# Inverted sums loaded as sixteen rows, and the order of the memory part changed, in a four-layer attention kernel on one Trainium2 core

## The chip, the cores and the metric

The kernel runs on one NeuronCore of one Trainium2 chip. Its engines are named as the profile names them: PE (TensorE, matmuls; PEld is its weight load), DVE (VectorE), ACT (ScalarE), POOL (GpSimd) and SP (SyncE, which here only issues DMAs). Sixteen DMA engines move data between the chip's memory and the on-chip memories. The metric is the device time of one execution in microseconds; the time before is the median of three executions.

## The reference, cut to what matters

The input x has 2048 tokens of 512 values, split into 32 heads of 16. Four layers run one after the other, A, B, A, B, with one set of weights for both A layers and one for both B layers. Everything is float32.

```python
def _A_ref(x, wqkv, w_phi, wo):            # linear attention
    ...
    phi_q = concatenate([softmax(pq), softmax(-pq)])
    phi_k = concatenate([softmax(pk), softmax(-pk)])
    kv = einsum("bhsf,bhsd->bhfd", phi_k, v); z = einsum("bhsf->bhf", phi_k)
    o = (phi_q @ kv) / (phi_q . z + 1e-6)
    return o @ wo

def _B_ref(x, wq, wk, wv, wo, beta):       # softmax attention in 4 segments with a memory
    ...
    for s in range(4):                     # 512 tokens each
        p = softmax(qs @ ks.T * scale + causal_mask)
        a_dot = p @ vs
        num = phi(qs) @ M;  den = phi(qs) . z + 1e-6
        o_s = g * (num / den) + (1.0 - g) * a_dot
        M = M + phi(ks).T @ vs;  z = z + sum(phi(ks))
    return concat(o_s) @ wo

x = x + A(layernorm(x)); x = x + B(layernorm(x)); x = x + A(layernorm(x)); x = x + B(layernorm(x))
```

An output of a B layer has two parts. The new part `a_dot` comes from the segment's own softmax and is divided by the row sums of the exponentials. The memory part `num / den` comes from the segments before, and is divided by a sum of its own. In the first segment there is no memory yet.

## The kernel before

**Tiles and loops.** Work is laid out with features on the 128 partitions for the B layers: a group `c` of the four groups of eight heads fills 128 partitions (8 heads x 16 features) and the 512 tokens of a segment lie along the free dimension. A B layer is walked by `steps` as 160 numbered steps `k`: 32 half groups `m` (segment `s = m // 8`, group `c = m % 8 // 2`, half `hf = m % 2`), with `R = 5` steps each. In every step `attend` makes one part of the scores of the present half group (PE), `exp` of them (ACT) and the causal mask on the diagonal blocks (POOL, the AFFINE_SELECT instructions on tile P); `maxima` makes row maxima of a later half group (PE into the banks mx and my, DVE); `weighted` makes the products with v (PE into the bank pv, ACT to tile U); `put_maxima` turns the maxima (PE), negates them (ACT) and writes them into the stacked q tile by a DMA that ACT issues (e<-mt).

**The order.** Each engine runs its instructions in the order in which the program emits them (`Ordered`, `held`), and that order is written by hand. The tables FIRST, GAPS, LAST and FINAL (lines 81 to 120) name the filler work of each step: FIRST for segment 0, GAPS for segments 1 and 2, LAST for segment 3 of the first B layer, FINAL for segment 3 of the second. A cell such as `1.3 q3/1~ k3/2` says: in step 3 of half group 1, one quarter of the projection q of group 3 (three matmuls of 512 columns), with the DVE part of its emptying put off into the next step (`~`), then two quarters of k of group 3. `n` normalises and turns rows of the next segment, `out` is the output projection, `x0` to `x3` ask for residual rows (`ask`, tile xr), `max` is `put_maxima`, `v` in LAST is work of the next A layer, and `a1`, `a2`, `a3`, `a0+` are `read` for a group of this or the next segment. TAIL (line 61) is the order of the last pieces of the kernel.

**The sums and their inverses.** For each segment and group, the sums by which outputs are divided are gathered in a DRAM buffer of 16 rows of 512 values (`den`): rows 0 to 7 for the new part of the eight heads (written by `gather`, four rows a half group, from tile U), rows 8 to 15 for the memory part (written by `dens` in `read`, four rows each from the tiles mmq and ot). `invert` then schedules four actions by the table INVERT: `compact` reads the buffer back as a full 128-partition tile (dn with both parts, 64 columns; dm with one part, 32 columns), `flip` takes the reciprocal on DVE, `put` writes it to DRAM (inv), and `load` reads the eight rows of a part back, each repeated for the 16 partitions of its head, as a 128 x 512 tile: KN for the new part, mmq for the memory part.

**The outputs.** `close` is called for a group when its second half is done, with the step number `k` from which the actions are counted, and schedules by the table JOIN: `scaled` (new part times KN, POOL, tmp<-tmp,KN), `scaled_old` (memory part times mmq, POOL, ot<-ot,mmq), `joined` (their sum, POOL, tmp<-tmp,ot), `upper` (ACT, oh<-tmp) and `lower` (POOL, ol<-tmp,oh), the two halves of the number with which the output projection is run. JOIN has one row for segment 0, one for segments 1 and 2, one for segment 3. A whole number of steps is run ahead of the filler of that step, a half one behind it. In segment 3, groups from `cut` = 2 on take another way (`finish`, `end_turn`, `close_last`), and their memory part is scaled by an action set in `read`.

**What `read` does.** It multiplies the memory with phi(q) (PE, into the bank pv and a bank g) and ACT empties the two banks into `old` (tile ot, three buffers) and `upper` (tile mmq, two buffers, which the loads of the memory part's inverses share). The pv bank is a single one, and the next `weighted` needs it.

**Queues.** Nearly all DMAs are issued by SP, in program order; ACT issues e<-mt.

The lines that place `scaled` and its companions are:

```python
            for j, f in zip(JOIN[0 if s == 0 else 2 if s == NSEG - 1 else 1][c], (scaled, scaled_old, joined, upper, lower)):
                if j is not None:
                    self.at(k + j, f)
```

Of the kernel before, what the change touches and what calls it, by code (L numbers as in the profile page):

```python
# [15 lines left out]
D = 512  # L16
H = 32
DH = 16
P = 128
# [29 lines left out]
GATHER = (3.5, 1.5)  # L49
INVERT = (((2.5, 4.5, 5, 7), (2.5, 4.5, 5, 7), (2.5, 4.5, 5, 7), (2.5, 4.5, 5, 7)), ((2.5, 5.0, 5, 7), (2.5, 5.0, 5, 7), (2.5, 5.0, 5, 7), (2.5, 5.0, 5, 7)), ((2.5, 4.5, 5.5, 7.5), (2.5, 4.5, 5.5, 7.5), (2.5, 4.5, 5.5, 7.5), (2.5, 4.5, 5.5, 7.5)))  # L50
READ = (1.5, 2.5, 1, 12.5)
JOIN = (((9.5, None, None, 11, 12.5), (9.5, None, None, 11, 12.5), (9.5, None, None, 11, 12.5), (9.5, None, None, 11, 12.5)), ((9.5, 10.0, 11.5, 12, 13.5), (9.5, 10.0, 11.5, 12, 13.5), (9.5, 10.0, 11.5, 12, 13.5), (9.5, 10.0, 11.5, 12, 13.5)), ((9.5, 11.5, 12.5, 13, 13.5), (9.5, 11.5, 12.5, 13, 13.5), (9.5, 11.5, 12.5, 13, 13.5), (9.5, 11.5, 12.5, 13, 13.5)))
SEAM = 1
QFIRST = False
WARM = 18
# [2 lines left out]
BEGINNING = """  # L58
m0 m1 g0 r0 n0 V0 n1a V1p c0 V2 V3p c1 m2 m3 v1 v1 v1 v1 g1 r1 p n2 k k v1 n3a v1 v1 v1 c2 k k c3 u k v1 v1 v1 K0 K1 K2 K3 v1 u u q q u q u v1 q v1 v1 u u u q Q0 Q2 v1 Q1 u Q3 u u
"""  # L60
TAIL = "p o0 p o1 o2 t0 p p p p o3 t2 P t1 a0 t3 a1 a2 a3"
WEIGHTS = {-2: ((0, (0, 3)), (1, (1, 2))), -1: ((-2, (0,)), (-1, (3, 1)), (0, (2,)))}
SECOND = 9
EARLY = (0, 1, 2)
# [25 lines left out]
"""  # L90
GAPS = """
0.1 max k2/3 | 0.2 n | 0.3 k2/1~ v3/2 | 0.4 a1 v3/2
1.0 m0 n n | 1.1 max q3/3 | 1.2 n | 1.3 q3/1~ k3/2 | 1.4 t1 k3/2~
2.1 max out/3 | 2.2 m1 | 2.3 ln ln | 2.4 a2 ln x0
3.1 max ln out/1~ | 3.3 q0+/3 x1 | 3.4 t2 q0+/1~ k0+/2
4.1 max k0+/2~ out/1 load | 4.2 m2 | 4.3 out/3~ x2 | 4.4 a3 q1+/4~
# [7 lines left out]
1.0 n | 1.1 max q3/3 n | 1.2 n | 1.3 q3/1~ k3/2 n | 1.4 k3/2~ n  # L104
2.1 max out/1 | 2.3 out/2 | 2.4 a2 x0 pre
3.1 max ln~ ln~ | 3.3 pre out/1 ln~ out/1 x1 | 3.4 out/1 ln~
4.1 max out/2~ v/3 | 4.3 pre out/3 x2 | 4.4 a3 out/1~ v/1 x3
5.1 max out/3 | 5.2 out/1 v/1 | 5.3 fin v/1 | 5.4 v/2 pre
6.1 v/2 max | 6.3 fin v/2 | 6.4 v/2
7.1 pt p/3 v/2 | 7.2 v/2 | 7.3 fin v/2 p/3 | 7.4 p/3  # L110
"""
FINAL = """
# [2 lines left out]
2.1 max k3/2 | 2.3 k3/1 out/1 pre | 2.4 a2 out/2 x0  # L115
3.0 x1 | 3.1 max | 3.3 pre out/2 | 3.4 out/2
4.1 max out/1~ | 4.3 pre out/2 x2 | 4.4 a3 out/2
5.1 max out/2 x3 | 5.3 fin out/2 | 5.4 pre
6.1 max | 6.3 fin
7.1 pt p/2 | 7.3 p/4 fin | 7.4 p/3  # L120
"""
# [4 lines left out]
def interleave_kernel(ctx, tc, x_in, a_wqkv, a_wphi, a_wo, b_wq, b_wk, b_wv, b_wo, b_beta,  # L126
# [15 lines left out]
    def nm(s):  # L142
        uid[0] += 1
        return f"{s}_{uid[0]}"

    def T2(tag, bufs, dt=F32, shape=(P, 512)):
        return sp.tile(list(shape), dt, tag=tag, bufs=bufs, name=nm(tag))

    def PS(tag, bufs, shape=(P, 512)):
        return ps.tile(list(shape), F32, tag=tag, bufs=bufs, name=nm(tag))  # L150
# [38 lines left out]
    dve, act, pool, sync = [Ordered(e) for e in (nc.vector, nc.scalar, nc.gpsimd, nc.sync)]  # L189
# [10 lines left out]
    def mm(*a, **k):  # L200
        n = a[0].free_size()
        work[0] += n / 2.26 if k["rhs"].dtype == F32R else (n * 2 / 2.4 + 25 if "tile_position" in k else 2 * max(112, n * 2 / 2.4))
        return held(nc.tensor.matmul(*a, **k))  # L203
# [55 lines left out]
    def dtile(shape, name):  # L259
        return dr.tile(list(shape), F32, name=name)  # L260
# [745 lines left out]
    class LayerB:  # L1006
# [69 lines left out]
        def read(self, s, c, k):  # L1076


            kn, ph = self.summed(s, c)[1], self.st[s, c]["phi", 0]
            pn = [PS("pv", PV), PS("g", G)]  # L1080
            for a in range(2):
                mm(pn[a][0:68, :], lhsT=kn[64 * a : 64 * a + 64, :], rhs=ph[64 * a : 64 * a + 64, :],
                   start=True, stop=True, tile_position=(64 * a, 0))
            old = self.old[s, c] = T2("ot", OT)
            upper = T2("mmq", 2)
            for t, p in zip((old, upper), pn):
                act.activation(t[0:68, :], p[0:68, :], AF.Identity, bias=bd[0:68, 26:27])

            def dens():
                d = self.den(s, c)  # L1090
                for a, t in enumerate((upper, old)):
                    sync.dma_start(out=d[12 - 4 * a : 16 - 4 * a], in_=t[64:68, :])

            def numerators():
                sync.dma_start(out=old[64:128, :], in_=upper[0:64, :])
            self.at(k + READ[0], dens)
            self.at(k + READ[1], numerators)
            if s == NSEG - 1 and c >= self.cut:
                self.invert(s, c, k + READ[2], range(1, 2), INVERT[2][c])

                def scaled():
                    pool.tensor_tensor(out=old, in0=old, in1=self.inv.pop((s, c, 1)), op=MUL)
                self.at(k + READ[3], scaled)

        def den(self, s, c):
            if (s, c) not in self.dens:
                self.dens[s, c] = dtile((16, D), nm("den"))
            return self.dens[s, c]

        def invert(self, s, c, k, parts, steps):  # L1110


            lo, hi = 8 * parts[0], 8 * parts[-1] + 8
            n = (hi - lo) * 4
            tiles = {}

            def compact():
                d = tiles["d"] = T2("dn" if n == 64 else "dm", 1, shape=(P, n))
                sync.dma_start(out=d[:, 0:n], in_=self.den(s, c)[lo:hi].rearrange("h (x i) -> (h x) i", i=n))

            def flip():
                dve.reciprocal(tiles["d"][:, 0:n], tiles["d"][:, 0:n])

            def put():
                tiles["i"] = dtile((hi - lo, D), nm("inv"))
                sync.dma_start(out=tiles["i"].rearrange("h (x i) -> (h x) i", i=n), in_=tiles["d"][:, 0:n])

            def load():
                for i in parts:
                    t = self.inv[s, c, i] = T2(*(("mmq", 2) if i else ("KN", 1)))  # L1130
                    rows = tiles["i"][8 * i - lo : 8 * i - lo + 8].unsqueeze(1).broadcast_to([8, DH, D])
                    sync.dma_start(out=t, in_=rows)
            for j, f in zip(steps, (compact, flip, put, load)):
                self.at(k + j, f)

        def gather(self, s, c, hf, U):
            if hf == 0:
                self.num[s, c] = T2("tmp", 2)
            sync.dma_start(out=self.num[s, c][64 * hf : 64 * hf + 64, :], in_=U[1 - hf : P : 2])
            sync.dma_start(out=self.den(s, c)[4 * hf : 4 * hf + 4], in_=U[31 * hf : P : 32])  # L1140

        def outputs(self, s, c):
            return [T2("oh", OO, F32R), T2("ol", OO, F32R)]
# [1 line left out]
        def close(self, s, c, k):  # L1145
# [19 lines left out]
            def lower():  # L1165
                hi, lo = self.oT[s, c]
                pool.tensor_tensor(out=lo, in0=o, in1=hi.bitcast(F32), op=SUB)
            for j, f in zip(JOIN[0 if s == 0 else 2 if s == NSEG - 1 else 1][c], (scaled, scaled_old, joined, upper, lower)):
                if j is not None:
# [189 lines left out]
        def close_last(self, rest):  # L1359
# [36 lines left out]

            for what in TAIL.split():
                if what == "p":
# [218 lines left out]
    for i in range(2):  # L1617
        lb = LayerB(xs[2 * i + 1], xs[2 * i + 2], CUTS[i], i == 1)
        run(p1[i])
        a2 = la[i].second  # L1620
# [41 lines left out]
```

## Time and profile before

| | us |
|---|---|
| median of three executions | 1423.88 |
| lowest and highest of them | 1420.51 and 1424.61 |
| the profiled execution, whole | 1420.89 |
| its span in the profile | 1419.2 |
| ACT busy, DVE busy, POOL busy | 810.0, 953.1, 733.8 |
| the first B layer, from its first e<-mt to its last output, about | 281 to 716 |
| the second B layer, about | 977 to 1412 |

How to read the profile: a row of the costliest groups has the source line, the engine, the operation, the tiles (out<-in), the shape, the count, then busy time and mean duration in ns, then the engine's idle time ahead of these instructions and what ended most of it. Source lines tell little here, since the helpers on lines 181, 203, 207 and 210 issue nearly everything; the tiles' names tell the instructions apart. A row of the chain of waits has a start, a length and what the time was spent on; a DMA in it counts from its issue to the moment that released the next. A row of the timeline has start, duration, engine, operation, tiles, shape and count, and in brackets the idle time before it and what ended it. A row of busy times by stretch has the stretch, its length, the busy time of PE, PEld, DVE, ACT and POOL with their instruction counts, the granted TensorE clock as a share of full speed, the mean busy share of the sixteen DMA engines, and the rate in GB/s.

### The profile page before, as it was taken

To read this page: it belongs to the slowest core of one execution; us is meant where nothing else is said; L and a number is where in the kernel's file an instruction comes from. 1 tells how busy PE (TensorE), PEld (TensorE's weight loads), DVE (VectorE), ACT (ScalarE), POOL (GpSimd) and SP (SyncE) were. 2 spreads that over 40 slices of the span, in tenths; PEclk is the share of its full clock that TensorE was granted. 3 is DMA by queue.
4 is the path that set the end of the run, shared out by engine and by line. 5 is a ranking of instruction groups with operands and counts; after the bars stand their busy time and mean duration, and the time that the engine had idled before them with its cause. 6 is when DMAs were issued, how large, how long until landed. Compare 5 with 4: busy or idle time off the path is not lost.

```text
span 1419.2 us, 33171 instructions
## 1 busy us (share of the span) xinstructions
PE 1373.8 (97%) x12070; PEld 946.3 (67%) x12070; DVE 953.1 (67%) x3028; ACT 810.0 (57%) x1246; POOL 733.8 (52%) x1073
## 2 busy tenths in 40 slices
PE   9999999999999999999999999999999999999997
PEld 7787778765666565665568887886656565666554
DVE  5766888677666556577546768958776665666663
ACT  5555345447676576566544434553666765765654
POOL 1678765325566556554524446641446565654543
PEclk9999999999999999999999999999999999999999
DMA  5369285536655546466640104854465565555541
GB/s 196 119 220 335 92 267 187 173 115 186 186 132 167 167 133 179 147 162 196 173 146 31 61 31 132 266 177 144 129 185 147 148 182 158 146 165 145 142 143 68
DMA packets 134898, 222.72 MB, mean 157 GB/s; under 512 B 26032, under 2 KB 39472, under 8 KB 134736
## 3 DMA queue, kind: packets, MB, share of 16 engines
q1 hardware_dynamic: 132768, 219.96, 52.0%
q8 instruction: 97, 1.59, 0.5%
q10 hardware_dynamic: 1968, 0.64, 0.2%
q14 instruction: 65, 0.53, 0.1%
HBM read 115.54 MB, written 41.55 MB: 111 GB/s over the span
## 4 chain that ended last, share of the span: by engine, by line
PE 74%; DVE 7%; ACT 6%; DMA 5%; POOL 4%; issue 2%; SPq 1%; ACTq 0%; DVEq 0%; POOLq 0%
PE g L203 45%; PE pv L203 8%; PE lg L203 8%; PE mx L203 4%; PE g L207 3%; ACT P L181 3%; PE my L203 3%; POOL P L181 2%; PE lg L207 2%; DMA e<-ta 1%; SPq L181 1%; DVE es L181 1%; POOL tb L181 1%; POOL tmp L181 1%; DVE junk L181 1%
## 5 line engine op out<-in xcount | busy, mean ns | idle before, releaser
L181 ACT ACTIVATE P<-lg 128x1024 f32<-128x1024 f32 x316 | 324.8, 1028 | 172.5 <-PE lg L203 152.0
L181 POOL TENSOR_SCALAR_AFFINE_SELECT P<-P 128x256 f32<-128x256 f32 (+1 forms) x448 | 190.1, 439 | 399.0 <-ACT P L181 394.8
L181 DVE CUSTOM_DVE_ANT_0 junk<-mx,mask 128x128 uint8<-128x128 f32 (+2 forms) x384 | 147.2, 421 | 116.3 <-PE my L203 86.8
L203 PE MATMUL g<-hh,wqk 128*128 128x512 f32 x512 | 185.2, 410 | 0.7 <-ACT mt L181 0.7
L203 PE MATMUL lg<-e,e 64*128 64x512 f32 (+1 forms) x1010 | 166.3, 387 | 12.3 <-ACT P L181 10.8
L203 PE MATMUL g<-w,oh 128*128 128x512 f32 x508 | 169.5, 414 | 0.5 <-ACT hh L181 0.4
L203 PE MATMUL pv<-P,v 128*32 128x512 f32 (+3 forms) x2048 | 165.1, 439 | 4.4 <-ACT ot L181 4.3
L181 DVE CUSTOM_DVE_ANT_0 mx<-mx,mask 128x512 f32<-128x512 f32 x128 | 89.1, 696 | 114.6 <-PE my L203 93.6
L203 PEld LDWEIGHTS lg<-e,e 64*128 64x128 f32 x1010 | 80.1, 184 | 109.9 <-issue 50.7
L203 PE MATMUL my<-e,e 63*128 63x256 f32 (+3 forms) x519 | 148.1, 345 | 4.3 <-DVE mxs L181 3.2
L203 PE MATMUL mx<-e,e 63*128 63x256 f32 (+3 forms) x519 | 147.0, 336 | 2.2 <-DVE mxs L181 1.9
L181 DVE CUSTOM_DVE_ANT_0 junk<-my,mask 128x128 uint8<-128x128 f32 (+2 forms) x384 | 146.7, 420 | 0.0
L203 PE MATMUL g<-w,hh 128*128 128x512 f32 x448 | 144.0, 402 | 0.3 <-ACT hh L181 0.3
L203 PEld LDWEIGHTS pv<-P,v 128*32 128x32 f32 x2048 | 53.6, 109 | 106.4 <-issue 93.9
L203 PEld LDWEIGHTS g<-hh,wqk 128*128 128x128 f32 x512 | 96.2, 188 | 32.3 <-issue 11.8
L203 PEld LDWEIGHTS g<-w,oh 128*128 128x128 f32 x508 | 87.9, 189 | 30.3 <-issue 13.2
L203 PE MATMUL g<-w,ol 128*128 128x512 f32 x254 | 101.2, 398 | 2.9 <-DVE ol L181 2.1
L203 PE MATMUL g<-hl,wqk 128*128 128x512 f32 x256 | 100.3, 392 | 0.0
L181 DVE DVE_READ_ACCUMULATOR2_ANT mxs<- 128x1 f32 x1024 | 100.1, 98 | 0.0
L203 PEld LDWEIGHTS mx<-e,e 63*128 63x128 f32 (+1 forms) x519 | 90.5, 186 | 11.1 <-DVE mxs L181 4.8
L203 PEld LDWEIGHTS g<-w,hh 128*128 128x128 f32 x448 | 80.3, 188 | 22.9 <-issue 6.3
L203 PEld LDWEIGHTS my<-e,e 63*128 63x128 f32 (+1 forms) x519 | 83.9, 185 | 16.9 <-DVE mxs L181 8.7
(189 smaller groups left out, 2835.9 us busy)
## 6 DMA issues: line engine op xcount, KB each, us to landing
e<-ta SPq DMA_DIRECT2D x384, 128.0 KB
wqk<-wqk SPq DMA_DIRECT2D x64, 512.0 KB
x<-x SPq DMA_DIRECT2D x48, 256.0 KB
xr<-x SPq DMA_DIRECT2D x32, 256.0 KB
x<-xr SPq DMA_DIRECT2D x28, 256.0 KB
tmp<-U SPq DMA_DIRECT2D x56, 128.0 KB
KN<-inv SPq DMA_DIRECT2D x28, 256.0 KB
pq<-tb SPq DMA_DIRECT2D x24, 256.0 KB
```

The source lines that it names most:

```text
L181: i = f(*a, **k)
L203: return held(nc.tensor.matmul(*a, **k))
L207: return held(nc.tensor.transpose(*a))
```

## The change

Four things are changed.

1. The buffer of sums holds each row twice (16 x 2 x 512): the writes of `gather` and `dens` repeat their source rows, `compact` and `put` move tiles of twice the width (dn of 128 columns, dm of 64), `flip` inverts twice as many values, and `load` reads sixteen rows, each repeated for eight partitions, where it read eight rows, each repeated for sixteen.
2. In JOIN `scaled_old` moves from 10.0 to 9.5 for segments 1 and 2, which puts it directly behind `scaled`, and from 11.5 to 10.5 for segment 3.
3. In the tables: one quarter of q in GAPS moves from step 1.3 to 1.2; in LAST a quarter of `v` moves from 4.1 to 4.4 and at 6.1 the maxima come ahead of `v`; in FINAL at 5.1 the order becomes residual, output quarters, maxima.
4. In TAIL `o3` moves one quarter (`p`) forward.

```diff
-JOIN = (((9.5, None, None, 11, 12.5), ... ), ((9.5, 10.0, 11.5, 12, 13.5), ... ), ((9.5, 11.5, 12.5, 13, 13.5), ... ))
+JOIN = (((9.5, None, None, 11, 12.5),) * 4, ((9.5, 9.5, 11.5, 12, 13.5),) * 4, ((9.5, 10.5, 12.5, 13, 13.5),) * 4)
...
-TAIL = "p o0 p o1 o2 t0 p p p p o3 t2 P t1 a0 t3 a1 a2 a3"
+TAIL = "p o0 p o1 o2 t0 p p p o3 p t2 P t1 a0 t3 a1 a2 a3"
...
 GAPS = """
-1.0 m0 n n | 1.1 max q3/3 | 1.2 n | 1.3 q3/1~ k3/2 | 1.4 t1 k3/2~
+1.0 m0 n n | 1.1 max q3/3 | 1.2 n q3/1~ | 1.3 k3/2 | 1.4 t1 k3/2~
...
 LAST = """
-4.1 max out/2~ v/3 | 4.3 pre out/3 x2 | 4.4 a3 out/1~ v/1 x3
+4.1 max out/2~ v/2 | 4.3 pre out/3 x2 | 4.4 a3 out/1~ v/2 x3
...
-6.1 v/2 max | 6.3 fin v/2 | 6.4 v/2
+6.1 max v/2 | 6.3 fin v/2 | 6.4 v/2
...
 FINAL = """
-5.1 max out/2 x3 | 5.3 fin out/2 | 5.4 pre
+5.1 x3 out/2 max | 5.3 fin out/2 | 5.4 pre
...
             def dens():
                 d = self.den(s, c)
                 for a, t in enumerate((upper, old)):
-                    sync.dma_start(out=d[12 - 4 * a : 16 - 4 * a], in_=t[64:68, :])
+                    sync.dma_start(out=d[12 - 4 * a : 16 - 4 * a], in_=t[64:68, :].unsqueeze(1).broadcast_to([4, 2, D]))
...
-                self.dens[s, c] = dtile((16, D), nm("den"))
+                self.dens[s, c] = dtile((16, 2, D), nm("den"))
...
-            n = (hi - lo) * 4
+            n = (hi - lo) * 8
...
             def compact():
-                d = tiles["d"] = T2("dn" if n == 64 else "dm", 1, shape=(P, n))
-                sync.dma_start(out=d[:, 0:n], in_=self.den(s, c)[lo:hi].rearrange("h (x i) -> (h x) i", i=n))
+                d = tiles["d"] = T2("dn" if n == P else "dm", 1, shape=(P, n))
+                sync.dma_start(out=d, in_=self.den(s, c)[lo:hi].rearrange("h u (x i) -> (h u x) i", i=n))
...
             def put():
-                tiles["i"] = dtile((hi - lo, D), nm("inv"))
-                sync.dma_start(out=tiles["i"].rearrange("h (x i) -> (h x) i", i=n), in_=tiles["d"][:, 0:n])
+                tiles["i"] = dtile((2 * (hi - lo), D), nm("inv"))
+                sync.dma_start(out=tiles["i"].rearrange("h (x i) -> (h x) i", i=n), in_=tiles["d"])
...
             def load():
                 for i in parts:
                     t = self.inv[s, c, i] = T2(*(("mmq", 2) if i else ("KN", 1)))
-                    rows = tiles["i"][8 * i - lo : 8 * i - lo + 8].unsqueeze(1).broadcast_to([8, DH, D])
+                    rows = tiles["i"][2 * (8 * i - lo) :][0:16].unsqueeze(1).broadcast_to([16, DH // 2, D])
                     sync.dma_start(out=t, in_=rows)
...
-            sync.dma_start(out=self.den(s, c)[4 * hf : 4 * hf + 4], in_=U[31 * hf : P : 32])
+            sync.dma_start(out=self.den(s, c)[4 * hf : 4 * hf + 4],
+                           in_=U[31 * hf : P : 32].unsqueeze(1).broadcast_to([4, 2, D]))
```

More of the change, by code (lines that the diff above doesn't have):

```diff
@@ L51 @@
 READ = (1.5, 2.5, 1, 12.5)
-JOIN = (((9.5, None, None, 11, 12.5), (9.5, None, None, 11, 12.5), (9.5, None, None, 11, 12.5), (9.5, None, None, 11, 12.5)), ((9.5, 10.0, 11.5, 12, 13.5), (9.5, 10.0, 11.5, 12, 13.5), (9.5, 10.0, 11.5, 12, 13.5), (9.5, 10.0, 11.5, 12, 13.5)), ((9.5, 11.5, 12.5, 13, 13.5), (9.5, 11.5, 12.5, 13, 13.5), (9.5, 11.5, 12.5, 13, 13.5), (9.5, 11.5, 12.5, 13, 13.5)))
+JOIN = (((9.5, None, None, 11, 12.5),) * 4, ((9.5, 9.5, 11.5, 12, 13.5),) * 4, ((9.5, 10.5, 12.5, 13, 13.5),) * 4)
 SEAM = 1
@@ L1113, in invert @@
             lo, hi = 8 * parts[0], 8 * parts[-1] + 8
-            n = (hi - lo) * 4
+            n = (hi - lo) * 8
             tiles = {}
             def compact():
-                d = tiles["d"] = T2("dn" if n == 64 else "dm", 1, shape=(P, n))
-                sync.dma_start(out=d[:, 0:n], in_=self.den(s, c)[lo:hi].rearrange("h (x i) -> (h x) i", i=n))
+                d = tiles["d"] = T2("dn" if n == P else "dm", 1, shape=(P, n))
+                sync.dma_start(out=d, in_=self.den(s, c)[lo:hi].rearrange("h u (x i) -> (h u x) i", i=n))
             def flip():
-                dve.reciprocal(tiles["d"][:, 0:n], tiles["d"][:, 0:n])
+                dve.reciprocal(tiles["d"], tiles["d"])
             def put():
-                tiles["i"] = dtile((hi - lo, D), nm("inv"))
-                sync.dma_start(out=tiles["i"].rearrange("h (x i) -> (h x) i", i=n), in_=tiles["d"][:, 0:n])
+                tiles["i"] = dtile((2 * (hi - lo), D), nm("inv"))
+                sync.dma_start(out=tiles["i"].rearrange("h (x i) -> (h x) i", i=n), in_=tiles["d"])
             def load():
```

## The prediction

> **What bounds the kernel now.** I read the front page first, then busy times by stretch, then what TensorE (PE) waited for in those stretches, then the chain of waits and the engines' timelines around the longest of these waits.
>
> ```profile
> span 1419.2 us, 33171 instructions
> ...
> PE 1373.8 (97%) x12070; PEld 946.3 (67%) x12070; DVE 953.1 (67%) x3028; ACT 810.0 (57%) x1246; POOL 733.8 (52%) x1073
> ...
> PE 74%; DVE 7%; ACT 6%; DMA 5%; POOL 4%; issue 2%; SPq 1%; ACTq 0%; DVEq 0%; POOLq 0%
> ```
>
> PE is the bound: 97% busy and 74% of the chain that ended last. The change removes no matmul, so it can only win back moments in which PE stands still. Where are they? The memory part runs in the second to fourth segment of each attention layer, at 425 to 716 us and 1120 to 1412 us. In the rows below the first two numbers are the length of the stretch and PE's busy time, and the last is the data rate in GB/s.
>
> ```profile
> 425.00:650.00 225.00, 219.60 (x1770) 135.57 (x1768) 145.45 (x587) 146.04 (x213) 128.41 (x206) 1.00 0.56 158
> 650.00:716.00 66.00, 61.48 (x430) 35.82 (x430) 38.02 (x139) 36.51 (x51) 28.91 (x46) 1.00 0.66 189
> ...
> 1120.00:1345.00 225.00, 219.99 (x1775) 135.87 (x1775) 143.01 (x581) 143.89 (x209) 128.62 (x202) 1.00 0.56 155
> 1345.00:1412.00 67.00, 61.16 (x444) 33.52 (x441) 35.84 (x138) 36.22 (x53) 30.45 (x50) 0.97 0.36 103
> ```
>
> PE's idle time there is 5.4 + 4.5 + 5.0 + 5.8 = 20.7 us: the ceiling of what these stretches can return. The view of PE's waits names part of it, first for 425 to 716, then from 1120 to the end (us in total, times, longest).
>
> ```profile
> PE lg L203 <- ACT P L181: 4.1, 8, 1.0
> PE pv L203 <- ACT ot L181: 2.5, 3, 1.1
> ...
> PE lg L203 <- DMA mmq<-inv: 0.7, 1, 0.7
> ```
> ```profile
> PE lg L203 <- ACT P L181: 4.3, 9, 0.9
> PE pv L203 <- ACT ot L181: 1.9, 4, 1.0
> PE g L207 <- ACT U L181: 1.2, 1, 1.2
> PE mx L203 <- DVE mxs L181: 1.1, 1, 1.1
> PE g L203 <- POOL ol L181: 0.6, 1, 0.6
> ```
>
> Two kinds matter: scores (lg) waiting for an exponential that ACT made late, and weighted values (pv) waiting for ACT to empty the bank that `read` filled (ACT's ot). Behind both stand the loads of the inverted sums and the POOL chain that uses them.
>
> **The change part by part.** *The sixteen-row load.* A load moves 128 x 512 x 4 bytes = 256 KB.
>
> ```profile
> L181 SPq DMA_DIRECT2D KN<-inv x28: 628/657/670, 338.0 to 1384.6; - x28
> L181 SPq DMA_DIRECT2D mmq<-inv x24: 585/619/649, 442.7 to 1390.6; - x24
> ```
> ```profile
> 694.75 5.68 DMA KN<-inv
> ```
> ```profile
> 972.78 2.48 DMA ot<-x
> ```
> ```profile
> 698.00:698.50 0.50, 0.50 (x4) 0.42 (x3) 0.00 (x0) 0.29 (x1) 0.00 (x0) 1.00 0.47 180
> 698.50:699.00 0.50, 0.50 (x4) 0.41 (x3) 0.00 (x0) 0.50 (x1) 0.00 (x0) 1.00 0.50 184
> ```
>
> The eight-row load on the chain took 5.68 us; ot<-x, the same 256 KB read in whole partitions, took 2.48. While this load and its partner for the memory part were most of what was in flight, the share of DMA time (the number before the rate) stood at 0.47 to 0.50, at about 182 GB/s: half the engines carried it, half stood idle. Sixteen rows instead of eight give twice as many equal pieces. If all sixteen engines then carry it at the same rate each, one load needs 262,144 / 364,000 = 0.72 us in place of 1.44, and a pair 1.44 in place of 2.88: 0.7 to 1.4 us off the landing. The bounds are nothing (the split stays) and 5.68 - 2.48 = 3.2 us (the crowd was of the load's own making). I take 1.4 for the pairs, the value that the rate gives.
>
> [...]
>
> What does an earlier landing release?
>
> ```profile
> 538.93 1.02 ACT L181 ACTIVATE P<-lg 128x1024 f32<-128x1024 f32 x1 [2.56 <-DMA mmq<-inv]
> ```
> ```profile
> 674.59 1.30 POOL L181 TENSOR_TENSOR tmp<-tmp,KN 128x512 f32<-128x512 f32 x1 [6.66 <-DMA mmq<-inv]
> ```
> ```profile
> 680.44 0.68 ACT L181 ACTIVATE ot<-pv,bd 68x512 f32<-68x512 f32 x1 [2.64 <-POOL tmp L181]
> ```
> ```profile
> 1372.48 0.69 DVE L181 TENSOR_TENSOR xr<-g,xr 128x512 f32<-128x512 f32 x1 [3.79 <-issue]
> ```
>
> ACT stood 2.56 us ahead of an exponential that reads nothing of mmq: its issue of the row maxima (`put_maxima`) queued in front of it, and that waited for the load. POOL stood 6.66 us ahead of `scaled`; everything behind it on POOL, `joined` included, was late, and ACT's ot at 680.44 waited 2.64 us for that `joined`, which is the 1.1 us stall of PE. At 1372.48 DVE stood 3.79 us in front of a residual (the row names no cause); its source had been asked for right behind an eight-row load, and PE's 1.1 us on mxs follows. I count the 0.7 on mmq<-inv, 0.8 of the 1.1 on mxs, the 1.1 stall on ot, and of the 8.4 us on ACT's exponentials the part with a late issue or a late bank behind it, about 3: in sum 5.6.
>
> *`scaled_old` directly behind `scaled` (JOIN).* The middle segments go from 10.0 to 9.5, the last from 11.5 to 10.5.
>
> ```profile
> 538.20 1.29 POOL L181 TENSOR_TENSOR tmp<-tmp,KN 128x512 f32<-128x512 f32 x1
> 540.03 0.77 POOL L181 TENSOR_SCALAR_AFFINE_SELECT P<-P 128x256 f32<-128x256 f32 x2 [0.53 <-ACT P L181]
> 540.76 1.28 POOL L181 TENSOR_TENSOR ot<-ot,mmq 128x512 f32<-128x512 f32 x1
> ...
> 543.13 1.27 POOL L181 TENSOR_TENSOR tmp<-tmp,ot 128x512 f32<-128x512 f32 x1
> ```
>
> Today POOL ends `scaled` at 539.5, idles 0.53 us for ACT, masks, and only then scales the memory part. Put ahead, the 1.28 us fill that hole, so `joined` starts 0.53 us earlier; the two masks come 0.75 us later, which the pv matmuls, a step or more behind, cover. Six more stalls on ot stand (2.5 + 1.9 - 1.1 = 3.3 us); 0.5 us each, with a floor of nothing, gives 2. `scaled_old` now needs mmq one POOL instruction after KN: if that load is late, masks and exponentials queue behind it; that is what the 6.66 us would grow by, and the faster pair is the cover.
>
> *The doubled sums.* Each `compact` tile doubles in width.
>
> ```profile
> L181 DVE RECIPROCAL dn<-dn 128x64 f32<-128x64 f32 x20 | 11.0, 548 | 0.4 <-DMA dn<-den 0.4
> ```
> ```profile
> L181 DVE RECIPROCAL dm<-dm 128x32 f32<-128x32 f32 x12 | 4.2, 348 | 2.2 <-DMA dm<-den 2.2
> ```
> ```profile
> 502.18 0.42 DVE L181 CUSTOM_DVE_ANT_0 junk<-mx,mask 128x256 uint8<-128x256 f32 x1 [1.52 <-PE my L203]
> ```
>
> From 32 to 64 columns a reciprocal costs 200 ns more, so 64 to 128 costs 400: 20 x 0.40 + 12 x 0.20 = 10.4 us more on DVE. After one that ran some 3 us earlier, DVE next stands idle 1.52 us at 502.18, waiting for PE, so I cost it at nothing; without that cover it is the whole 10.4. The writes of the sums go from 8 to 16 KB, compact and put from 32 to 64 (16 to 32 in the short form); no row shows their price, and against the 256 KB of a load in 0.7 to 1.4 us I bound them at 0 to 0.1 us each, on transfers that end before the reciprocal. Their issue on SP could grow by at most the 0.66 us of KN<-inv, a broadcast too; I take 0.
>
> *The tables.* The q quarter moved to 1.2 takes three matmuls out of step 1.3, which also holds two k quarters; PE lists no wait there in the first of these places (412 to 426 us), so nothing, give or take 0.5 us at each of four. FINAL 5.1 asks for the residual ahead of the maxima and LAST 6.1 does the maxima first; both pull a waited-for item forward, and the two quarters of projection or output they trade places with keep PE fed: 0 to 1 us, I take 0.3. LAST moves a quarter of v by three steps, nothing. TAIL puts o3 one quarter earlier at the exposed end: 0.3, with the 0.6 on ol halved by `joined`: 0.3 more.
>
> **Sum.** 5.6 + 2.0 + 0.3 + 0.6 = 8.5 us. PE runs its queue in order, and what is released runs into the next wait: exponentials, maxima and POOL are each within a step of it. I take off two fifths, from the fact that only half of the idle 20.7 us is touched: about 5 us. The profiled execution took 1420.89 us with 1.7 around its span, 3.0 below the median of 1423.88; 1420.9 - 5 = 1415.9 on its scale, **1418.9** on that of the median.
>
> **Rivals.** *It was hidden anyway.* For it: ACT stood 2.56 us ahead of 538.93 and PE shows no wait of that length, because queued projections ran on. Against it: the stalls on ot do reach PE. Then only `joined` counts: -1 us, 1423.
>
> *The whole crowd clears.* If the halves of DMA even out, e<-ta, xr and the rest land earlier too, and three fifths of the 20.7 us return: -12, 1412. For it: rates of 180 GB/s at half the share; against it: stalls by DVE and PE's own order remain.
>
> *DVE becomes the late one.* The reciprocal sits between two groups of row maxima; both PSUM banks of the maxima stand behind it. If its extra 0.4 us exceeds the slack (it decides wherever the idle time after it is under 0.4 us), PE's next maxima start late. With half of the 10.4 us reaching PE and the gain of the loads cancelled by their own hidden share, +5: 1429. Against it: the 1.52 us.
>
> *The load doesn't spread.* The source is still one small buffer read many times. Then only JOIN and tables remain, -2: 1422; I give this together with the hidden case.
>
> **How the numbers follow.** No change means within 0.3%, 4.3 us, about what a measurement of this kernel can tell. Forecast 0.56, of which 0.42 below 1419.6 and 0.14 inside; the crowd clears 0.14, all faster; hidden or not spread 0.15, inside but for 0.02; DVE 0.15, of which 0.13 slower and 0.02 inside. So faster 0.56, same 0.29, slower 0.15. The range runs from 1411 (just past the crowd) to 1428 (all but the worst half of the DVE case); the forecast's own is 1415 to 1423.
>
> **What would show it.** KN<-inv and mmq<-inv landing near 3 us with a DMA share well above 0.5 while they fly; the 6.66 us ahead of `scaled` and the 2.56 ahead of P reduced to under half; ot<-ot,mmq directly behind tmp<-tmp,KN; PE's wait for ACT ot from 4.4 us to about 1; the 128-column reciprocal at 948 ns with PE's waits on mxs unchanged. I am wrong if PE's idle time in the four stretches falls by less than 2 us, or if the waits on mxs grow.

## The result, and the profile after

Six runs of the changed kernel took 1411.25 us in the median (1410.54 to 1412.43); six of the kernel before, beside them, 1421.62 (1416.73 to 1424.61). The ratio is 0.9933, 95% interval 0.9917 to 0.9950: 0.7% faster, 10.4 us by the medians. The prediction's forecast was 5 us; the time lies 0.25 us inside the low edge of its range (1411 to 1428), below the forecast's own (1415 to 1423). The profiled execution took 1410.82 us. Its page, in the rows that answer to those of before:

```profile
span 1409.1 us, 33171 instructions
...
PE 1371.5 (97%) x12070; PEld 944.2 (67%) x12070; DVE 959.9 (68%) x3028; ACT 809.9 (57%) x1246; POOL 734.6 (52%) x1073
...
PE 74%; DVE 8%; ACT 7%; POOL 5%; issue 3%; DMA 2%; SPq 1%; DVEq 0%; POOLq 0%; ACTq 0%
```

Span less PE's busy time is PE's idle time: 1419.2 - 1373.8 = 45.4 us before, 1409.1 - 1371.5 = 37.6 now, so 7.8 of the span's 10.1 us are idle time that went away. DMA's share of the chain went from 5% to 2%. DVE is 6.8 us busier and that shows nowhere. The next view gives the busy times of the four stretches in which the memory part runs. Their edges are those of before, moved by about as much as the work beside them came earlier (0 at 425 us, 2.6 at 650, 5.9 at 716, 5.3 at 1120, 7.8 at 1345, 9.6 at 1412).

```profile
425.00:647.40 222.40, 219.46 (x1769) 135.17 (x1767) 147.15 (x583) 146.01 (x213) 127.86 (x206) 1.00 0.59 163
647.40:710.10 62.70, 60.05 (x428) 35.11 (x428) 39.13 (x137) 35.93 (x49) 28.83 (x46) 1.00 0.70 203
1114.70:1337.20 222.50, 220.10 (x1777) 135.50 (x1778) 145.19 (x580) 143.41 (x210) 128.33 (x202) 1.00 0.59 161
1337.20:1402.40 65.20, 60.17 (x444) 33.43 (x440) 37.00 (x138) 36.48 (x54) 30.69 (x50) 1.00 0.39 110
```

PE's idle time here was 20.7 us and is 2.9 + 2.7 + 2.4 + 5.0 = 13.0. The third number from the right, the granted clock, is 1.00 in all four; in the last stretch of before it was 0.97. What PE waited for, from 425 to 716 us and then from 1115 us to the end (total, times, longest):

```profile
PE lg L203 <- ACT P L181: 2.9, 8, 0.6
PE mx L203 <- DVE mxs L181: 0.9, 1, 0.9
PE my L203 <- DVE mxs L181: 0.7, 3, 0.3
PE g L207 <- ACT U L181: 0.3, 1, 0.3
```
```profile
PE lg L203 <- ACT P L181: 3.2, 9, 0.9
PE g L207 <- ACT U L181: 1.2, 1, 1.2
...
PE pv L203 <- ACT ot L181: 0.5, 1, 0.5
```

The waits of the weighted values (pv) for ACT's ot were 2.5 + 1.9 = 4.4 us and are 0.5. The waits for exponentials (P) were 4.1 + 4.3 = 8.4 and are 6.1. On POOL, the timeline shows the three multiplications and additions of one set as the change orders them:

```profile
535.53 1.29 POOL L181 TENSOR_TENSOR tmp<-tmp,KN 128x512 f32<-128x512 f32 x1
536.77 1.29 POOL L181 TENSOR_TENSOR ot<-ot,mmq 128x512 f32<-128x512 f32 x1
...
539.87 1.29 POOL L181 TENSOR_TENSOR tmp<-tmp,ot 128x512 f32<-128x512 f32 x1
```

`scaled_old` follows `scaled` at once, and `joined` starts 4.34 us after `scaled`, where it was 543.13 - 538.20 = 4.93. The long wait ahead of `scaled` in the last segment, 6.66 us before, is still there, though:

```profile
670.45 1.29 POOL L181 TENSOR_TENSOR tmp<-tmp,KN 128x512 f32<-128x512 f32 x1 [5.20 <-DMA e<-ta]
```

The row names an e<-ta, since two semaphores moved at nearly the same time; by the semaphores' records KN<-inv landed at 670.28 us, 0.17 us before `scaled` began, and `scaled` needs KN. So POOL still waits for the load here, which is the first sign that the loads are not where the gain came from.

### The profile page after: what moved, and what is told of

The parts are those of the page before. It is cut to its first block, busy times and chain, and to the rows that moved or that the text cites. A ratio compares the mean times of both kernels' runs of the same rounds, so it can differ in the third digit from the quotient of the medians.

```text
span 1409.1 us, 33171 instructions
## 1 busy us (share of the span) xinstructions
PE 1371.5 (97%) x12070; PEld 944.2 (67%) x12070; DVE 959.9 (68%) x3028; ACT 809.9 (57%) x1246; POOL 734.6 (52%) x1073
## 4 chain that ended last, share of the span: by engine, by line
PE 74%; DVE 8%; ACT 7%; POOL 5%; issue 3%; DMA 2%; SPq 1%; DVEq 0%; POOLq 0%; ACTq 0%
PE g L203 46%; PE lg L203 8%; PE pv L203 8%; PE mx L203 4%; ACT P L181 3%; PE g L207 3%; PE my L203 3%; POOL P L181 2%; PE lg L207 2%; POOL tmp L181 1%; DVE es L181 1%; POOL ot L181 1%; ACT tb L181 1%; DVE my L181 1%; DVE junk L181 1%
## 5 line engine op out<-in xcount | busy, mean ns | idle before, releaser
L203 PEld LDWEIGHTS mx<-e,e 63*128 63x128 f32 (+1 forms) x519 | 90.7, 185 | 10.1 <-DVE mxs L181 4.9
```

## A ledger for all runs

Two things account for the span of every kernel in this study: PE's idle time, and moments in which PE's granted clock is half. Here are stretches of 3.4 us, first of before, then of the experiment after_eight_rows (below); the third number from the right is the clock, the first after the length is PE's busy time.

```profile
1372.30:1375.70 3.40, 2.04 (x10) 1.24 (x11) 2.69 (x8) 1.73 (x3) 3.22 (x4) 1.00 0.27 92
1375.70:1379.10 3.40, 3.40 (x15) 1.69 (x17) 1.66 (x8) 0.83 (x1) 0.06 (x1) 0.51 0.49 135
```
```profile
623.60:627.00 3.40, 0.91 (x14) 0.51 (x8) 0.63 (x2) 1.58 (x2) 1.75 (x3) 1.00 0.47 142
627.00:630.40 3.40, 3.40 (x13) 2.49 (x10) 2.25 (x10) 1.63 (x3) 2.29 (x4) 0.50 0.13 25
630.40:633.80 3.40, 3.40 (x20) 2.02 (x20) 1.96 (x9) 2.13 (x4) 0.64 (x1) 1.00 0.54 175
```

After these two stretches, in which PE stood still for 1.4 and 2.5 us in all, the clock was half for 3.4 us: in the second case 13 matmuls passed where the next stretch has 20. PE counts as busy for all 3.40 us of both, so an idle-time reading misses the cost, 0.5 x 3.4 = 1.7 us each time. Below, "half clock" is the time lost that way, summed over slices of 1 us up to 8 us before the end.

```
profiled run       span   PE busy  idle  half clock  rest    ACT held
before            1419.2  1373.8   45.4     1.7     1372.1    19.9
after             1409.1  1371.5   37.6     0.0     1371.5    10.8
after_again       1411.6  1372.8   38.8     1.7     1371.1    10.6
join_tables       1411.4  1372.2   39.2     1.7     1370.5    11.7
put_twice         1412.7  1372.5   40.2     1.7     1370.8    13.4
join_only         1412.7  1372.1   40.6     0.0     1372.1    18.8
loads_only        1413.3  1371.5   41.8     0.0     1371.5     9.5
tables_only       1414.2  1371.4   42.8     0.0     1371.4    13.2
last_only         1419.5  1374.9   44.6     3.4     1371.5    18.1
spread_only       1421.4  1375.1   46.3     3.4     1371.7    16.5
wide_dve          1423.5  1374.0   49.5     1.7     1372.3    20.6
late_loads        1425.4  1374.9   50.5     5.1     1369.8    17.8
after_eight_rows  1425.5  1376.2   49.3     3.4     1372.8    34.8
doubled_only      1428.2  1375.0   53.2     3.4     1371.6    30.6
```

The rest stays within 1369.8 to 1372.8 us: PE's own work, the same in all to within 3 us. So a change here pays or costs mostly what it does to idle time, and to the number of half-clock stretches. From before to after: 7.8 of idle, 1.7 of half clock, 0.6 of rest.

The last column is one kind of stall on ACT, added up over the 64 issues of the row maxima (e<-mt): the time between ACT's copy of the maxima (mt<-g) and its issue of their transfer, as far as it exceeds 0.05 us, during which no exponential runs. Its cause is in the semaphores: by the traces of before and after, the program's 1227 transfers use eight of them in turn (153 or 154 transfers each), and in before, after, doubled_only and after_eight_rows all 60 stalls of this kind over 0.5 us ended 0.08 us after the landing of the transfer that had the issue's semaphore before it. The transfer waited for has nothing to do with the maxima; most often it is an e<-ta of 128 KB (11 of 16 in before, 6 of 9 in after).

## The experiments

Each edit is one part of the change put into the kernel before, or one part of it taken out of the changed kernel. None leaves a part of the computation out. Ratios are to the kernel before, run in turn on the same chip, and an effect given in us is the ratio's, unless two medians stand beside it.

**The parts alone.** The diffs are against before. loads_only has the doubled sums and the sixteen-row load, and the old orders:

```diff
-                self.dens[s, c] = dtile((16, D), nm("den"))
+                self.dens[s, c] = dtile((16, 2, D), nm("den"))
...
-                    rows = tiles["i"][8 * i - lo : 8 * i - lo + 8].unsqueeze(1).broadcast_to([8, DH, D])
+                    rows = tiles["i"][2 * (8 * i - lo) :][0:16].unsqueeze(1).broadcast_to([16, DH // 2, D])
```

> Only the doubled sums and the sixteen-row load; JOIN, the step tables and TAIL as before. Theory L (the landing of the loads is what PE waited on, through POOL's scaled and ACT's late issues): 6 to 8 us faster than before, ratio 0.9945 to 0.996; KN<-inv and mmq<-inv land earlier and the 6.66 us ahead of scaled shrink. Theory J (the place of scaled_old carries it): 1 to 3 us faster at most. Theory T (the tables carry it): no change within 2 us. If the wider reciprocal costs PE time, it shows here as a gain smaller than L says, or a loss.

Measured: 1417.28 us against 1419.91, ratio 0.9988 (0.9976 to 1.0000), some 1.7 us: much less than the 5.6 us that the prediction gave to the loads. join_only has the new JOIN alone:

```diff
-JOIN = ( ... ((9.5, 10.0, 11.5, 12, 13.5), ... ), ((9.5, 11.5, 12.5, 13, 13.5), ... ))
+JOIN = ( ... ((9.5, 9.5, 11.5, 12, 13.5),) * 4, ((9.5, 10.5, 12.5, 13, 13.5),) * 4)
```

> Only JOIN changed: scaled_old at 9.5 in segments 1 and 2, at 10.5 in segment 3; loads with eight rows. Theory L: 1 to 2 us faster, ratio 0.9986 to 0.9993, since half of the stalls on ACT's ot remain with the late loads; the rival within it: slower by 1 to 3 us, because scaled_old stands on POOL for a memory load that has not landed and masks queue behind it. Theory J: 5 to 8 us faster, PE's wait for ACT ot near 1 us.

Measured: 1415.44, ratio 0.9975 (0.9964 to 0.9987), 3.5 us. PE's waits from 425 to 716 us show where it works:

```profile
PE lg L203 <- ACT P L181: 4.6, 8, 1.6
...
PE pv L203 <- ACT ot L181: 0.5, 1, 0.5
```

The wait on ot falls from 2.5 to 0.5 us with the old, slow load; the exponentials stay as late as before (4.6 after 4.1). tables_only has GAPS, LAST, FINAL and TAIL:

```diff
-1.0 m0 n n | 1.1 max q3/3 | 1.2 n | 1.3 q3/1~ k3/2 | 1.4 t1 k3/2~
+1.0 m0 n n | 1.1 max q3/3 | 1.2 n q3/1~ | 1.3 k3/2 | 1.4 t1 k3/2~
...
-6.1 v/2 max | 6.3 fin v/2 | 6.4 v/2
+6.1 max v/2 | 6.3 fin v/2 | 6.4 v/2
...
-5.1 max out/2 x3 | 5.3 fin out/2 | 5.4 pre
+5.1 x3 out/2 max | 5.3 fin out/2 | 5.4 pre
```

> Only GAPS, LAST, FINAL and TAIL changed. Theories L and J: within 1.5 us of before, ratio 0.999 to 1.001. Theory T: 3 us or more faster, seen in segments 1 and 2 of both layers (the moved q quarter) or at the seam and the end (LAST, FINAL, TAIL).

Measured: 1416.94, ratio 0.9980 (0.9964 to 0.9996), 2.8 us, where the prediction had 0.6 for these edits with the tail. The three parts sum to 8.0 us; the whole change gave 0.9933 and, run again below, 0.9941, which is 9.5 and 8.4 us. They add up about as they stand, as far as the intervals tell: no sign that anything was given back.

**The load's rows.** after_eight_rows is the changed kernel, reading every second of the sixteen rows, so that eight rows feed sixteen partitions each as before, out of the doubled buffer:

```diff
-                    rows = tiles["i"][2 * (8 * i - lo) :][0:16].unsqueeze(1).broadcast_to([16, DH // 2, D])
+                    rows = tiles["i"][2 * (8 * i - lo) : 2 * (8 * i - lo) + 16 : 2].unsqueeze(1).broadcast_to([8, DH, D])
```

> The changed kernel, but load reads every second of the sixteen rows, eight rows each repeated for sixteen partitions as before; sums still doubled, JOIN and tables as changed. Theory L: most of the gain is gone, 1414 to 1419 us on the scale on which the changed kernel takes 1411, with scaled_old now standing for the late memory load. Theory J or T: within 2 us of the changed kernel. The wider reciprocal and the doubled writes are in it, so it can't be better than join_only and tables_only together unless these are free.

Measured: 1423.96, ratio 1.0038 (1.0023 to 1.0054), slower than before in spite of the new orders. Going from sixteen rows back to eight cost some 14 us on the ratios' scale, more than the whole change had brought. Its timeline of ACT at the longest of PE's stalls:

```profile
620.38 0.25 ACT L181 ACTIVATE mt<-g 16x128 fp32r<-16x128 f32 x1
624.79 0.53 ACTq L181 DMA_DIRECT2D e<-mt  x1
625.42 1.02 ACT L181 ACTIVATE P<-lg 128x1024 f32<-128x1024 f32 x1 [4.79 <-DMA e<-ta]
```

ACT had the maxima at 620.63 and could issue their transfer only at 624.79, when an e<-ta issued at 618.58, right behind KN<-inv and mmq<-inv, had landed. The exponential behind it, for which the scores had been ready since 624.05, began at 625.42. PE stood from 624 to 626.5 and ran at half clock from 627.0 to 630.4 (the rows of the ledger).

**The parts in pairs.** after_again is the changed kernel once more, join_tables the changed kernel with the sums and loads of before, doubled_only the kernel before with doubled sums and the load of after_eight_rows, and put_twice the changed kernel with single sums, whose inverses are written twice:

```diff
-                sync.dma_start(out=tiles["i"].rearrange("h (x i) -> (h x) i", i=n), in_=tiles["d"])
+                for u in range(2):
+                    sync.dma_start(out=tiles["i"].rearrange("(h u) (x i) -> u h x i", u=2, i=n)[u], in_=tiles["d"][:, 0:n])
```

> The changed kernel once more, on the chip of the three beside it and with their runs of before. All theories: ratio 0.9917 to 0.995 as before, 1410 to 1414 us. It is the reference for the other three.

> JOIN, step tables and TAIL as changed; sums and loads as before (eight rows, not doubled). Theory A (the parts simply add; doubling the sums is what made the eight-row run slow): 5 to 7 us faster than before, ratio 0.995 to 0.9965. Theory I (the new order needs early loads: scaled_old and the moved maxima stand for a transfer that lands late, wherever it does): 0 to 3 us faster, or slower, with POOL waiting on mmq<-inv and ACT on late issues as in the eight-row run.

> Only the sums are doubled (writes, compact, reciprocal, put); the load reads eight rows; JOIN and tables as before. Theory A: 5 to 11 us slower than before, ratio 1.0035 to 1.008, since the wider reciprocal (10.4 us more on DVE) or the larger transfers reach PE. Theory I: within 2 us of before; PE's waits on mxs as before.

> The changed kernel, but the sums are not doubled: sums, compact and reciprocal are as before, and put writes each inverse twice, by two transfers, for the same sixteen-row load. Theory A: 3 to 8 us faster than the changed kernel, 1403 to 1409, since the doubling's cost goes and the spread stays. Theory I (the doubling is hidden): within 2 us of the changed kernel, since 10 us less on DVE buys nothing and one more transfer a group is issued by SP.

Measured, against 1421.04: after_again 1412.50 (0.9941, 0.9924 to 0.9959), join_tables 1413.93 (0.9952, 0.9935 to 0.9969), put_twice 1413.97 (0.9951, 0.9934 to 0.9968), doubled_only 1431.22 (1.0079, 1.0058 to 1.0099). So the orders alone bring 4.8 of the 5.9 parts in a thousand; the loads add 1.4 us to them by the medians, which the intervals don't tell from nothing; and the same spread without doubling adds nothing at all. Doubling without the spread costs 11 us under the old orders, and 12 under the new (after_eight_rows against join_tables). The waits of PE in doubled_only from 425 to 716 us:

```profile
PE lg L203 <- ACT P L181: 8.2, 13, 1.2
PE pv L203 <- ACT ot L181: 3.3, 5, 1.4
```

Exponentials were late 13 times in place of 8, for 8.2 us in place of 4.1. The landing times, from the semaphores' records between 425 and 1412 us (median, 90th percentile and longest of each kind, in us from the issue), with the part of ACT's stalls that ended on an e<-ta:

```
                   KN<-inv            mmq<-inv           e<-ta             ACT held by e<-ta
before             4.47  5.86  8.38   5.49  7.44  9.02   3.62  5.98  8.52        11.7
after              3.89  4.88  6.90   4.33  5.46  7.36   3.32  5.04  7.03         8.2
doubled_only       4.66  6.19  9.31   6.40  7.85 10.18   3.75  6.33  9.68        22.1
after_eight_rows   4.75  6.09 10.01   6.38  7.34 10.51   3.94  6.13 10.15        23.7
put_twice          3.86  5.51  7.38   4.36  5.67  7.70   3.40  5.30  7.34         9.4
spread_only        3.73  5.88  8.01   4.46  6.19  8.36   3.37  5.62  7.82         6.8
```

Read from the doubled buffer in eight rows, mmq takes 0.9 us longer than before; the loads of ta that are in flight beside it land later, the late ones most; and the time for which they hold ACT doubles. With sixteen rows all of this reverses.

**What lateness, spread and DVE cost by themselves.** Three theories stood here: that an earlier landing of the two loads pays in itself (A); that the loads have a deadline, so that late costs and early pays little (D); and that the price of doubling is DVE's time (V). spread_only is before with the inverses put twice and the sixteen-row load; wide_dve is before with a second reciprocal, of a scratch tile, behind each real one; late_loads is before with the loads half a step later; last_only is before with the two edits of LAST. Diffs against before (spread_only's is that of put_twice and the load of loads_only):

```diff
+                dve.reciprocal(spare[:, 0:n], full[:, 0:n])
```
```diff
-INVERT = (((2.5, 4.5, 5, 7), ... ), ((2.5, 5.0, 5, 7), ... ), ((2.5, 4.5, 5.5, 7.5), ... ))
+INVERT = (((2.5, 4.5, 5, 7.5), ... ), ((2.5, 5.0, 5, 7.5), ... ), ((2.5, 4.5, 5.5, 8.0), ... ))
```
```diff
-4.1 max out/2~ v/3 | 4.3 pre out/3 x2 | 4.4 a3 out/1~ v/1 x3
+4.1 max out/2~ v/2 | 4.3 pre out/3 x2 | 4.4 a3 out/1~ v/2 x3
-6.1 v/2 max | 6.3 fin v/2 | 6.4 v/2
+6.1 max v/2 | 6.3 fin v/2 | 6.4 v/2
```

> Before, with the sixteen-row load alone: sums, compact and reciprocal single, put writes each inverse twice; JOIN, tables and TAIL as before. Theory A (costs add: doubling +10, spread -12): about 1409, ratio 0.990 to 0.993. Theory D (a deadline: the doubling makes the chain from sums to scaled later, the spread makes it earlier, and only lateness costs, so earliness pays little): ratio 0.995 to 0.999, 1 to 6 us faster.

> Before, with a second reciprocal of 64 or 32 columns on a scratch tile directly behind each real one: 20 x 0.55 + 12 x 0.35 = 15 us more on DVE, half as much again as the wider reciprocal brought, and the chain of put and load not delayed. Theory V (what the doubling costs with the eight-row load is DVE's time): 7 to 15 us slower, PE's waits on mxs grow. Theory D: within 2 us of before.

> Before, with each load of inverses issued half a step later (last column of INVERT plus 0.5), which puts it behind that step's filler; nothing else. Theory D: 3 to 10 us slower, with POOL's waits ahead of scaled and ACT's late issues grown as in the run with doubled sums alone. Theory V or A: within 2 us of before.

> Before, with the edits of LAST alone (a quarter of v moved from 4.1 to 4.4, maxima ahead of v at 6.1). If these carry the tables' gain: 1.5 to 3 us faster, all of it between 656 and 716 us of the first B layer. If the q quarter, FINAL or TAIL carry it: within 1 us of before.

Measured, against 1420.20: spread_only 1421.58 (1.0005, 0.9995 to 1.0016), wide_dve 1422.11 (1.0015, 1.0004 to 1.0025), late_loads 1424.91 (1.0027, 1.0013 to 1.0042), last_only 1417.12 (0.9969, 0.9957 to 0.9982).

spread_only: theory A falls. Its loads are faster in flight (table above), and the time does not move. Theory D, which had foreseen a small gain, is too high as well. POOL's waits from 425 to 1412 us say why:

```profile
POOL tmp L181 <- DMA KN<-inv: 8.1, 3, 6.6
```

These waits were 6.7 + 1.1 us in before (the first under the name of mmq<-inv). POOL still waits 6.6 us ahead of `scaled` in its worst place: SP has one transfer more to issue ahead of the load and issues it 0.45 us later, so KN lands within 0.1 us of where it did. (Such shifts are means from 425 to 1412 us, against the starts of ACT's exponentials on either side of each load.) wide_dve: theory V falls. Its extra reciprocals (the group by tile; min, median, max in ns) are longer than what doubling adds to the real ones:

```profile
L181 DVE RECIPROCAL spare<-full x32: 289/493/496, 337.1 to 1389.6; 128x64 f32<-128x64 f32 x20, 128x32 f32<-128x32 f32 x12
```

They cost 2 us; doubling costs 11. late_loads: half a step later costs 4 to 5 us, so lateness does cost. But its KN lands 2.3 us late and its mmq 1.5, while in doubled_only they land only 0.4 and 0.8 late. The waits that grow are others, too: from 425 to 716 us PE's waits for exponentials are 4.1 us in late_loads, as in before, and those on ot grow from 2.5 to 4.7; in doubled_only it is the exponentials that grow, to 8.2. So lateness of `scaled` can make only a part of the 11 us. The stalls of ACT are of the size: 30.6 us in doubled_only and 34.8 in after_eight_rows, against 19.9 in before and 17.8 in late_loads, and PE's worst stall in after_eight_rows stands right behind one of them (the rows above). How much of the 11 us each stall carries was not measured one by one.

last_only: the two edits bring 4.4 us (3.1 by the medians), at least all that tables_only brought. Which of the two does it can be read from the profile, since they act at different times. The first instructions that differ from before are the three matmuls of the moved quarter; the new order in 6.1 first shows in the turning of the maxima, at 699.53 us in before and 698.64 in last_only. Up to there, PE's waits are, in before (656 to 698 us) and in last_only (660 to 698):

```profile
PE pv L203 <- ACT ot L181: 1.1, 1, 1.1
PE mx L203 <- DVE mxs L181: 0.8, 2, 0.5
PE lg L203 <- DMA mmq<-inv: 0.7, 1, 0.7
PE my L203 <- DVE mxs L181: 0.5, 2, 0.3
PE g L207 <- ACT mt L181: 0.2, 1, 0.2
```
```profile
PE lg L203 <- ACT P L181: 0.6, 1, 0.6
PE g L207 <- ACT mt L181: 0.2, 1, 0.2
PE my L203 <- DVE mxs L181: 0.2, 1, 0.2
```

That is 3.3 us in before and 1.0 in last_only. Of the difference 0.4 us lies ahead of the first instruction that differs, and so is not the edit's. Behind 698 us PE waits 0.7 us in before and 0.3 in last_only. So the moved quarter saves about 1.9 us of idle time here and the order in 6.1 about 0.4. The longest of the waits shows how, first in before, then in last_only:

```profile
679.63 0.40 PE L203 MATMUL my<-e,e 63*128 63x512 f32 x1
681.18 1.28 PE L203 MATMUL pv<-P,v 128*32 128x512 f32 x16 [1.15 <-ACT ot L181]
```
```profile
681.90 0.62 PE L203 MATMUL g<-w,hh 128*128 128x512 f32 x2
682.35 0.39 PE L203 MATMUL g<-w,hl 128*128 128x512 f32 x1
...
683.34 1.29 PE L203 MATMUL pv<-P,v 128*32 128x512 f32 x16
```

The quarter that was run in step 4.1 now stands in step 4.4, behind the memory products of `read`, where PE used to wait for ACT to empty their bank (ot). It covers that wait. The other kernels agree: in this place PE waits 0.50 to 2.61 us for ot in the seven profiles without the edits of LAST, and nowhere over 0.15 us in the seven with them.

## Why the prediction came out as it did

**Right: what bounds it.** PE's idle time in four stretches was the thing to win, and 7.7 of the 20.7 us there were won, with no wait in the place of those removed.

**Right in mechanism, too small: JOIN.** The hole of 0.53 us on POOL was filled, `joined` came 0.59 us earlier relative to `scaled`, the masks' delay showed nowhere, and the waits on ot fell from 4.4 to 0.5 us. The term was 2.0 us; alone the edit measured 3.5. It priced six stalls of 3.3 us in all at 0.5 us each, less a floor; they went almost whole (4.4 us of waits on ot are 1.2 with JOIN alone).

**Wrong: the 5.6 us for the sixteen-row load.** This is the step that failed: "I count the 0.7 on mmq<-inv, 0.8 of the 1.1 on mxs, the 1.1 stall on ot, and of the 8.4 us on ACT's exponentials ... about 3". The load's own part was right. It does spread: while the pair is in flight with a tb<-x, the share of DMA time is near 1 (0.99 in the row below), where the prediction had seen 0.47 to 0.50.

```profile
692.50:693.00 0.50, 0.50 (x14) 0.21 (x6) 0.50 (x2) 0.00 (x0) 0.41 (x1) 1.00 0.99 311
```

The median flight of KN fell by 0.58 us and of mmq by 1.16, inside the 0.7 to 1.4 that the prediction had estimated from the share of 0.47 to 0.50, or just below. But the working left out that the doubled chain ahead of the load is longer. Of the sums' rows, those from ot land 2.34 us after their issue in place of 1.60 and those from mmq 2.33 in place of 1.92 (those from U no later), where the prediction's bound was 0.1 us more. SP takes 0.68 us to issue a den<-ot and took 0.29, for which the prediction put 0. And the reciprocal, which the load waits for, is longer by the 0.4 us that the prediction priced, but only as DVE's time:

```profile
L181 DVE RECIPROCAL dn<-dn x20: 945/948/953, 439.7 to 1368.2; 128x128 f32<-128x128 f32 x20
```

So the write of the inverses is issued 0.60 us later and the KN load 0.45; KN lands only 0.28 us earlier, mmq 1.29 (against ACT's exponentials, as above). In doubled_only these two issues are 0.53 and 0.31 us later, in join_tables, with single sums, -0.01 and 0.05: the delay comes with the doubling. Of the prediction's signs, the 2.56 us on ACT at 538.93 went (that issue now follows the copy of the maxima after 0.03 us), but POOL's 6.66 us became 5.20, not under half. The 1.1 us stall on ot is 0.50 with the loads alone and with JOIN alone, and gone with LAST alone. The parts alone give the loads 1.7 us.

**Wrong: doubling costs nothing.** DVE's extra time is indeed hidden: PE's waits on mxs from 425 to 716 us are 0.9 + 0.7, and were 0.8 + 0.9. But the cover for doubling is not DVE's 1.52 us; it is the sixteen-row load. Without it doubling costs 11 us; that it does so through transfers that land later and hold ACT fits the stalls, but was not tested by itself. Doubling and spread are one edit that nearly breaks even: it costs 11 to 12 us and gives 13 to 15.

**Wrong: the tables at 0.3.** "LAST moves a quarter of v by three steps, nothing": the edits of LAST bring 3 to 4 us, and by the profile most of it is this quarter. The order in 6.1, which the prediction priced with FINAL at 0 to 1 us, is of that size. The prediction looked at the very place, POOL at 674.59 and ACT at 680.44, and saw one way out of PE's 1.1 us there, an earlier load. Work for PE while ACT is late is another, and needs no load.

**Wrong: two fifths off.** Nothing was visibly given back. The parts sum to 8.0 us, and the whole gives 8.4 to 10.4. That the sum before the deduction, 8.5, lies so near is luck: its largest term was three times too large, two others too small. That the time lies inside the range is luck of the same kind: its edge of 1411 was drawn for the rival "the crowd clears".

**Missed: the clock.** The 0.97 in the prediction's fourth stretch is the 1.7 us of half clock, and no step of it used that. A sum over idle time alone is short by that.

Of the rivals, "hidden anyway" was right about the loads, and wrong about the whole, because the orders did not depend on them. "The crowd clears" had the time (1412) and half the reason: the other transfers do land earlier (e<-ta 5.98 to 5.04 at the 90th percentile), though most of the gain stands without that.

What stays open: why eight rows out of the doubled buffer take 0.9 us longer for mmq than out of the single one. doubled_only differs from before in the buffer's size, in the wider writes ahead of the load and in reading every second row, and no run separated the three. The two edits of LAST were not run apart either; how they divide is read from one profile of each kernel.

## What to carry to other kernels

Here KN flew 0.58 us less and landed only 0.28 us earlier, since what lies ahead of the load had become longer: work out the landing time of the whole chain, not of its last link, and ask who waits at that landing. Reordering work was worth more here than the transfer (4.8 of 5.9 parts in a thousand), and is tested alone in one run: put `scaled_old` into a hole of POOL, or a quarter of v where PE stands waiting for ACT. Where a wait ends on a transfer that the waiting work doesn't read, look for a queue or semaphore that they share.

## What the runs showed of the hardware

**Half clock after short stalls.** The trace of before records the clock at 0.50 from 1375.74 us on for 3.413 us. In after_eight_rows two such stretches began at 627.0 and 681.6 us, 16.0 times 3.413 apart; in spread_only at 688.0 and 1377.5, 202.0 times. These four lasted 3.4 us each; in late_loads one lasted twice that, from 686.7 to 693.5 us. A stretch of 3.4 us with 2.04 us of PE work was followed by half clock (before, 1372.3 us). PE's busy time alone doesn't decide it: in late_loads this stretch, with less, was followed by one at 1.00.

```profile
1246.40:1249.80 3.40, 1.56 (x18) 0.68 (x18) 1.22 (x4) 3.07 (x5) 0.71 (x2) 1.00 0.70 154
1249.80:1253.20 3.40, 3.14 (x22) 1.85 (x20) 2.55 (x13) 2.02 (x4) 1.77 (x3) 1.00 0.45 101
```

Much of the spread between runs of one kernel goes with this. Sorted by their mean granted clock, the runs of before, over all groups, give (one run, recorded at 0.949 without a longer time, is left out):

```
mean clock   1.000    0.999    0.998    0.997    0.996
runs           26       32       12        4        2
median us   1418.8   1420.3   1422.5   1424.2   1425.2
```

The median rises by 1.6 us for each 0.001 of the mean clock, which by a straight line through these 76 runs goes with half of the variance of their times. One stretch of half clock is 1.7 / 1419 = 0.0012 of the mean clock. All six first runs of the changed kernel stood at 1.000, and three of six later ones; of doubled_only none did (0.998 to 0.994). The changed kernel's two sets of six runs spread over 1.9 and 2.1 us, the six of doubled_only over 7.6.

**Eight semaphores for 1227 transfers.** All 60 stalls of issues on ACT over 0.5 us, in four profiles, ended 0.08 us after a landing that the issue's data does not need. In before that held ACT for 19.9 us in all, in the changed kernel for 10.8.
